# Converting the MoE weights in half-width VectorE steps inside the attention

## The chip, the core and the metric

The kernel runs on one core of a Trainium2 chip. The metric is the time of one execution on the device, in microseconds (us); the profile is one such execution. The core has five engines, each of which takes its instructions strictly in the order in which the program wrote them: TensorE (PE; its weight loads have a row of their own, PEld), VectorE (DVE), ScalarE (ACT), GpSimd (POOL) and SyncE (SP), which here only issues transfers (DMA). An engine that waits for a semaphore holds up all that is queued behind it.

## What is computed

```python
# attention: 2 batches x 8 heads, 768 positions, 64 wide, 16 clusters
q_assign = argmax(normalize(q) @ normalize(c).T); k_assign likewise
mask     = q_assign[:, :, :, None] == k_assign[:, :, None, :]
scores   = where(mask, q @ k.T / 8, -1e9)
attn     = softmax(scores);  x = attn @ v          # (1536, 512) after the heads are joined
# first MoE layer: float64-wide inputs read as given, 512 -> 2048 -> 512
h = x @ w_in;  x = elu(h) @ w_out
# second: 4 experts, 512 -> 1024 -> 512
out = sum_e p[:, e] * (relu(x @ w1[e]) @ w2[e])
```

The weights w_in and w_out come as 64-bit floats. [...]

## The kernel before

The attention runs first, then the two MoE layers. The attention goes over 48 windows w; six windows make a pair of heads, and a window handles two blocks of 128 query rows. All instructions of all windows are sorted by a table of numbers: a step with the name N of window w stands at AT[N] + 4.6 w, plus a correction from SHIFT for the window's place in its pair (w mod 6). This sort is the order in which each engine gets its work; nothing reorders it later. The numbers are units of that table, not microseconds.

The steps of a window that matter here:

- S0, S1: TensorE's scores into PSUM (L364, L367). M0, M1: VectorE's row maximum of each (L373). E0, E1: ScalarE's exponential with the row sum (L382).
- G0, R0: the sum plus 1e-9 (ScalarE, L390) and its reciprocal (VectorE, L394). P0, P1: GpSimd scales the rows by it (L400).
- T0 to T2: TensorE's transposes (L412). C0 to C2: ScalarE's copies to ph, the high part (L425; some to raw, L422). L0 to L2: VectorE's low part pl (L433), in four of 18 cases GpSimd's (L430, L431).
- V0, V1: TensorE's product with v (L441). X0, Y0: one head's half is copied (ScalarE, L453) and added to xs (VectorE, L461). Z0: GpSimd's split of xs (L472, L473).
- Q0 to Q5: the preparation of the next pair (transposes qkps, copies qh and kh L201, low parts L203, cluster logits lps L239 and L240, one-hot rows ohps and ohT L287, and SyncE's transfers of these into the operands QA, QB, KA, KB).
- W0, at 3.79: one step of the weight conversion, from window 3 on.

The conversion (`weights`, L484, and `w_split`, L683) is a generator. Each time do_W is called it runs to the next yield. Two weight chunks are converted inside the attention, each in two halves of 128 x 512 numbers, with one buffer for the raw words (w_raw) and one for the two intermediate tiles (w_tmp). A half's ten steps are: the load by SyncE (L626 or L629); an empty one; Abs of the high words by ScalarE (L702); a clamp by VectorE (L704, TENSOR_SCALAR); a shift with xor by VectorE (L707, TENSOR_SCALAR) with ScalarE's Sign (L708); the low words' three bits shifted in by VectorE (L710, SCALAR_TENSOR_TENSOR); Abs by ScalarE (L714); the sign multiplied back by VectorE (L716, TENSOR_TENSOR); the high part by ScalarE (L718); the low part by GpSimd (L721). The other 14 chunks are converted in the MoE stage, at twice that width, by the same w_split without the small buffers.

Of the kernel before, what the change touches and what calls it, by code (L numbers as in the profile page):

```python
# [8 lines left out]
F32 = mybir.dt.float32  # L9
# [4 lines left out]
AF = mybir.ActivationFunctionType  # L14
ALU = mybir.AluOpType
# [8 lines left out]

PERIOD = 4.6
AT = dict(
    S0=0, M0=0.23, Q0=0.36, Q1=0.85, S1=1.23, Q2=1.45, Q3=1.49, E0=1.75, Q4=3.28, M1=3.78, W0=3.79,
    Q5=4.23, E1=5.04, G0=5.64, R0=6.1, P0=6.11, P1=7.19, T0=10.42, C0=10.63, T1=11, T2=11.5,
    L0=12.79, C1=13.17, C2=13.81, L1=13.84, L2=14.94, V0=17.59, V1=19.11, X0=19.59, Y0=20.28, Z0=20.57,
)  # L30
SHIFT = {
    ("E1", 0): -0.35, ("E0", 1): 1.04, ("V0", 1): 0.84, ("S0", 2): -2.55, ("W0", 2): -3.28, ("G0", 4): 0.41, ("R0", 4): 0.41, ("P0", 4): 0.41,
    ("V1", 4): -1.31, ("W0", 4): 2.64, ("V0", 5): 1.42,
}

POOL_SPLITS = (2, 4, 6, 11)
# [5 lines left out]
TOP = float.fromhex("0x1.cp+16")  # L42
LOW = float.fromhex("0x1.2p-15")
# [3 lines left out]
def kernel(  # L47
# [14 lines left out]
    pe, act, dve, pool, sp = nc.tensor, nc.scalar, nc.vector, nc.gpsimd, nc.sync  # L62
# [28 lines left out]
    def gtile(tag, name, shape, dt):  # L91
        t = gen.tile([128, 1024], dt, tag=tag, name=name)
        n = 1
        for x in shape[1:]:
            n *= x
        if len(shape) == 2:
            return t[:shape[0], :n]
        names = "abcd"[:len(shape) - 1]
        return t[:shape[0], :n].rearrange(
            f"p ({' '.join(names)}) -> p {' '.join(names)}", **dict(zip(names, shape[1:]))  # L100
        )


    def attention():
# [145 lines left out]
        def prep_argmax(j, part, g0=0, g1=4):  # L250

            yield
            yield
            n = g1 - g0
            if part == 0 and g0 == 0:
                oh_t[j] = (
                    am_p.tile([128, T, 4, 1], F32, tag="mx", name="mx"),
                    am_p.tile([128, T, 4, C], F32, tag="rk", name="rk"),
                    am_p.tile([128, T, 4, C], BF16, tag="oh", name="oh"),
                )  # L260
            if n == 4:
                L, mx, rk, oh = (x.rearrange("p t g c -> p (t g) c") for x in (L_t[j], *oh_t[j]))
            else:
                L, mx, rk, oh = (x[:, :, g0] for x in (L_t[j], *oh_t[j]))
            top = mx.to_broadcast([128, T * n, C])
            if part == 0:
                dve.tensor_reduce(out=mx, in_=L, axis=AX.X, op=ALU.max)
                eng = dve if j == 0 else pool
                eng.tensor_tensor(out=L, in0=L, in1=top, op=ALU.subtract)
            elif part == 1:  # L270
                dve.scalar_tensor_tensor(
                    out=rk, in0=L, scalar=0.0, in1=ramp.to_broadcast([128, T * n, C]), op0=ALU.is_ge, op1=ALU.mult
                )
                dve.tensor_reduce(out=mx, in_=rk, axis=AX.X, op=ALU.max)
            else:
                dve.tensor_tensor(out=oh, in0=rk, in1=top, op=ALU.is_equal)
# [31 lines left out]
        def run(*gens):  # L308
            for g in gens:
                for _ in g:  # L310
                    pass
# [172 lines left out]
        def weights(n):  # L484

            for i in range(2):
                raw = cv_p.tile([128, 512, 2], I32, tag="raw", name="w_raw")
                w_load(n, [raw], i)
                yield
                yield  # L490
                tmp = cv_p.tile([128, 2, 512], I32, tag="tmp", name="w_tmp")
                yield from w_split(n, [tmp[:, x] for x in range(2)], i)
# [1 line left out]
        w_gen = [g for n in range(W0) for g in (weights(n),)]  # L494

        def do_W(w, i):
            if w < 3:
                return
            while w_gen:
                if next(w_gen[0], 0) is None:  # L500
                    return
                w_gen.pop(0)
# [34 lines left out]
        for nm in "qk":  # L537
# [7 lines left out]
        NW = NPAIR * 2 * NH  # L545
        do = dict(S=do_S, M=do_M, E=do_E, G=do_G, R=do_R, P=do_P, T=do_T, C=do_C, L=do_L, V=do_V, X=do_XC, Y=do_XA,
                  Z=do_XS, Q=do_Q, W=do_W)

        items = sorted(
# [3 lines left out]
        for at, w, nm in items:  # L553
            if w == 0 and nm == "S0":
                run(*(prep_argmax(0, i, g, g + 1) for i in range(3) for g in (1, 3)))
# [47 lines left out]
    A11, A12, A22, S1, S2, S3, S4 = range(7)  # L603
    W0 = 2
# [8 lines left out]
    def w_tiles(n):  # L613
        return [home(f"{t}{n % NSLOT}", [128, 2, 512], f"w{t}{n % NSLOT}") for t in "hl"]
# [37 lines left out]
    def w2_split(n):  # L652

        st = st_t.pop(n).bitcast(F32).rearrange("p i f t -> p i (f t)")
        a, b = st[:, 0], st[:, 1]
        tags = W2_TAGS[n % 2]
        a = a.rearrange("p (k c f) -> p k c f", k=KD, c=2)
        b11, b12, b21, b22 = (a[:, k:k + 2, c] for k in (0, 2) for c in range(2))
        t = gen.tile([128, 4, 2, 128], F32, tag="kh", name="T")
        dve.tensor_tensor(out=t[:, 0], in0=b12, in1=b11, op=ALU.subtract)  # L660
        dve.tensor_tensor(out=t[:, 2], in0=b22, in1=b12, op=ALU.subtract)
        yield
        dve.tensor_tensor(out=t[:, 1], in0=t[:, 0], in1=b22, op=ALU.subtract)
        dve.tensor_tensor(out=t[:, 3], in0=t[:, 1], in1=b21, op=ALU.add)
        yield
        ops = {}
        for x, names in (
            (a[:, :, 0], ("B11", "B21")), (t[:, 0:2].rearrange("p a k f -> p (a k) f"), ("T1", "T2")),
            (t[:, 2:4].rearrange("p a k f -> p (a k) f"), ("T3", "T4")), (b22, ("B22",)),
        ):  # L670
            m = 2 * len(names)
            o = home(tags[len(ops) // 2], [128, 2, m, 128], "w1op")
            yield from split(o[:, 0], o[:, 1], x, dve)
            for i, nm in enumerate(names):
                ops[nm] = [[o[:, z, 2 * i + kk] for kk in range(2)] for z in range(2)]
            yield
        h, l = (home(tag, [128, 2, 512], "w2op") for tag in tags[4:])
        b = b.rearrange("p (c d) -> p c d", c=2)
        yield from split(h, l, b, dve)
        w_t[n] = ops, (h, l)  # L680
        yield

    def w_split(n, tmp=None, half=None):  # L683
        if chunks[n][0] == 2:
            yield from w2_split(n)
            return
        a = st_t.pop(n)
        if n not in w_t:
            w_t[n] = w_tiles(n)
        h, l = w_t[n]  # L690
        if half is not None:
            h, l = h[:, half], l[:, half]

        small = tmp is not None
        a32, sg = tmp if small else [gtile(("qh", "kl", "kh")[n % 3], "wa", [128, 2, 512], I32), gtile("ql", "wsg", [128, 2, 512], I32)]
        at = (slice(None),) * (len(a.shape) - 1)
        hi, lo = a[at + (1,)], a[at + (0,)]
        x, sg = a32.bitcast(F32), sg.bitcast(F32)  # L700

        act.activation(out=x, in_=hi.bitcast(F32), func=AF.Abs)  # L702
        yield
        dve.tensor_scalar(x, x, LOW, TOP, ALU.max, ALU.min)  # L704
        if small:
            yield
        dve.tensor_scalar(a32, a32, 3, 0x40000000, ALU.logical_shift_left, ALU.bitwise_xor)  # L707
        act.activation(out=sg, in_=hi.bitcast(F32), func=AF.Sign)  # L708
        yield
        dve.scalar_tensor_tensor(  # L710
            out=a32, in0=lo, scalar=29, in1=a32, op0=ALU.logical_shift_right, op1=ALU.bitwise_or
        )
        yield
        act.activation(out=x, in_=x, func=AF.Abs)  # L714
        yield
        dve.tensor_tensor(out=x, in0=x, in1=sg, op=ALU.mult)  # L716
        yield
        act.activation(out=h, in_=x, func=AF.Copy)  # L718
        if small:
            yield  # L720
        pool.tensor_tensor(l, x, h.bitcast(F32), ALU.subtract)  # L721
        yield

    def moe():
# [254 lines left out]
        def tick(t, k=1):  # L979
            for n in start.get(t, ()):  # L980
                w_gen2[n] = w_split(n)
                going.append(w_gen2[n])
            for _ in range(k):
                going[:] = [it for it in going if next(it, 0) is None]
            for n in load_at.get(t, ()):
                w_load(n)
# [68 lines left out]
```

## Time and profile before

| | us |
|---|---|
| median of 3 runs | 1052.17 (1049.82 to 1054.71) |
| the profiled execution | 1049.63 |
| its span, first to last instruction | 1047.9 |
| TensorE busy | 1029.1 |
| VectorE busy | 735.4 |
| ScalarE busy | 524.2 |
| GpSimd busy | 392.8 |
| attention's steady part | 26 to 262 |

The span is what the trace covers; the rest of the execution's time, 1.73 us, lies around it. Busy times are read by stage, since the engines' shares differ from stage to stage. Matmuls are pipelined and their ends are modelled, so a TensorE that is busy isn't one at its peak. The chain of work that ended last is followed back from the last instruction: each piece is what the next one had waited for, or what stood ahead of it on its engine.

### The profile page before, as it was taken

The page shows a single profiled execution, that of the slowest core. Times are in us where ns is not written, and L with a number is a line of the kernel's source. Part 1 is how long each engine was busy: PE and PEld are TensorE (multiplying, and loading weights), DVE is VectorE, ACT ScalarE, POOL GpSimd, SP SyncE. Part 2 cuts the span into 40 slices and gives each one's busy share as a digit, 9 for nine tenths or more (in the row PEclk, how much of TensorE's full clock was granted, in tenths as well). Part 3 has the DMA queues.
Part 4 walks back from the last instruction along what each step waited for, and adds up shares of the span by engine and source line. Part 5 has one row for each costly group of instructions (what it writes and reads, how often), then busy time and mean ns, then how long its engine had stood idle before and what let it go on. Part 6 is the DMA issues. An engine that isn't in the chain of part 4 may idle for free.

```text
span 1047.9 us, 16446 instructions
## 1 busy us (share of the span) xinstructions
PE 1029.1 (98%) x6253; PEld 918.4 (88%) x6253; DVE 735.4 (70%) x1248; ACT 524.2 (50%) x1081; POOL 392.8 (37%) x394
## 2 busy tenths in 40 slices
PE   8999999999999999999999999999999999999998
PEld 7989999989877888888888898999999898989897
DVE  6999989998689674326576765666666767666665
ACT  4989999988676563324442332233332333332331
POOL 2888888889578766344641000000000000000000
PEclk8999999999999999999999999999999999999999
DMA  8746664431323221010002101111101111001003
GB/s 184 186 109 155 144 145 104 111 92 33 114 96 122 81 96 66 1 41 0 1 1 81 41 1 41 41 41 41 35 7 41 41 42 41 17 25 41 1 1 121
DMA packets 61790, 67.53 MB, mean 64 GB/s; under 512 B 29008, under 2 KB 47440, under 8 KB 61712
## 3 DMA queue, kind: packets, MB, share of 16 engines
q1 hardware_dynamic: 61712, 66.49, 22.4%
q8 instruction: 49, 0.80, 0.3%
q14 instruction: 29, 0.24, 0.1%
HBM read 43.08 MB, written 3.15 MB: 44 GB/s over the span
## 4 chain that ended last, share of the span: by engine, by line
PE 84%; DVE 8%; ACT 4%; issue 2%; DMA 1%; SPq 1%; POOL 1%; DVEq 0%; ACTq 0%; POOLq 0%
PE a L915 35%; PE h L765 23%; PE h L745 10%; PE x L441 5%; PE tps L412 4%; PE s L364 2%; PE s L367 2%; DVE pl L433 2%; DVE nm L373 1%; PE lps L239 1%; PE lps L240 1%; DVE wa L710 1%; ACT ph L425 1%; PE qkps L199 1%; ACT e L382 1%
## 5 line engine op out<-in xcount | busy, mean ns | idle before, releaser
L765 PEld LDWEIGHTS h<-x,w1op 128*128 128x128 f32 x2016 | 257.4, 190 | 10.3 <-ACT r L776 1.2
L765 PE MATMUL h<-x,w1op 128*128 128x256 f32 x2016 | 261.2, 285 | 1.0 <-ACT r L776 1.0
L915 PE MATMUL a<-w2op,gh 128*128 128x512 f32 x768 | 238.4, 392 | 0.0
L915 PEld LDWEIGHTS a<-w2op,gh 128*128 128x128 f32 x768 | 138.0, 188 | 23.9
L924 DVE SCALAR_TENSOR_TENSOR acc<-a,prob,acc 128x512 f32<-128x512 f32 x180 | 129.7, 746 | 40.2 <-PE a L915 40.2
L915 PE MATMUL a<-w2op,gl 128*128 128x512 f32 x384 | 149.8, 390 | 0.0
L745 PE MATMUL h<-xT,wh 128*128 128x512 f32 x384 | 118.5, 390 | 0.6 <-DVE gg L754 0.5
L400 POOL TENSOR_SCALAR p<-e,sm 128x768 f32<-128x768 f32 x96 | 88.4, 927 | 40.2 <-DVE sm L394 29.0
L754 DVE SCALAR_TENSOR_TENSOR gg<-r,h 128x512 f32<-128x512 f32 x48 | 32.9, 685 | 96.5 <-ACT r L753 75.4
L373 DVE TENSOR_REDUCE nm<-s 128x1 f32<-128x768 f32 x96 | 90.9, 947 | 2.8 <-PE s L367 2.6
L382 ACT ACTIVATE e<-s,nm 128x768 f32<-128x768 f32 x96 | 86.6, 902 | 4.5 <-POOL p L400 2.8
L412 PE MATMUL tps<-ident,p 128*128 128x128 f32 x576 | 83.5, 277 | 2.9 <-DVE pl L433 2.7
L745 PEld LDWEIGHTS h<-xT,wh 128*128 128x128 f32 x384 | 71.9, 188 | 16.2 <-DVE gg L754 1.4
L776 ACT ACTIVATE r<-h 128x256 f32<-128x256 f32 x48 | 18.4, 384 | 134.8 <-PE h L765 134.8
L915 PEld LDWEIGHTS a<-w2op,gl 128*128 128x128 f32 x384 | 72.1, 188 | 15.6
L433 DVE TENSOR_TENSOR pl<-tps,ph 128x512 fp32r<-128x512 f32 x112 | 76.2, 683 | 6.6 <-ACT ph L425 5.2
L441 PE MATMUL x<-ph,v 128*128 128x256 f32 x288 | 76.6, 298 | 1.4 <-DVE xs L461 1.3
L752 ACT ACTIVATE r<-h 128x512 f32<-128x512 f32 x48 | 28.6, 595 | 97.7 <-PE h L745 96.9
L915 PE MATMUL a<-gh,wh 128*128 128x512 f32 x192 | 74.9, 390 | 1.0 <-ACT acc L931 0.9
L755 POOL TENSOR_SCALAR gh<-gg 128x512 fp32r<-128x512 f32 x48 | 41.0, 854 | 92.0 <-DVE gg L754 89.2
L915 PE MATMUL a<-gl,wh 128*128 128x512 f32 x192 | 74.8, 390 | 0.0
L915 PE MATMUL a<-gh,wl 128*128 128x512 f32 x192 | 74.7, 389 | 0.0
(152 smaller groups left out, 1942.1 us busy)
## 6 DMA issues: line engine op xcount, KB each, us to landing
st<-in_moe_w_dram SPq DMA_DIRECT2D x32, 512.0 KB, 4.3
st<-in_moe_w_in_dram SPq DMA_DIRECT2D x14, 512.0 KB, 3.7
st<-in_moe_w_out_dram SPq DMA_DIRECT2D x14, 512.0 KB, 4.6
QA<-qh SPq DMA_DIRECT2D x32, 192.0 KB, 4.2
nq<-in_q_dram SPq DMA_DIRECT2D x16, 192.0 KB, 3.8
nk<-in_k_dram SPq DMA_DIRECT2D x16, 192.0 KB, 3.9
nv<-in_v_dram SPq DMA_DIRECT2D x8, 384.0 KB, 3.9
QB<-ql SPq DMA_DIRECT2D x16, 192.0 KB, 4.2
```

The lines of the kernel that those rows point to most:

```text
L373: dve.tensor_reduce(out=m_t[w][:, i:i + 1], in_=s_t[HALF * w + i][:, :, 0:384], axis=AX.XY, op=ALU.max, negate=True)
L382: act.activation(out=e, in_=s_t.pop(u)[:, :, 0:384], func=AF.Exp, bias=m_t[w][:, i:i + 1], accum_out=e_t[w][0][:, i:i + 1])
L400: pool.tensor_scalar(p, e_t[w][1 + i].rearrange("p a b -> p (a b)"), e_t[w][0][:, i:i + 1], 1.0, ALU.mult, ALU.mult)
L412: pe.transpose(ps[:, x, :], p_t[w][i][:, c * 128:(c + 1) * 128], ident)
L433: dve.tensor_tensor(out=l, in0=ps, in1=h.bitcast(F32), op=ALU.subtract)
L441: pe.matmul(x_t[w], lhsT=v2[j][:, r, c, :], rhs=t[:, :, c, :], start=(c == 0 and t is ph[w]), stop=(c == T - 1 and t is pl[w]),)
L745: pe.matmul(ps, lhsT=w[:, 0, f], rhs=x, start=(kk == 0 and i == 0), stop=(kk == KD - 1 and i == 2))
L754: dve.scalar_tensor_tensor(out=gg, in0=r, scalar=-1.0, in1=ps, op0=ALU.add, op1=ALU.max)
L755: pool.tensor_scalar(gh, gg, 1.0, 0.0, ALU.mult, ALU.add)
L765: pe.matmul(ps, lhsT=w[wz][kk], rhs=x[xz][:, kk], start=(start and kk + i == 0), stop=(stop and kk == 1 and i == 2), skip_group_check=True,)
L915: pe.matmul(ps, lhsT=x, rhs=y, start=(opens and i == 0), stop=(closes and i == len(ops) - 1))
L924: dve.scalar_tensor_tensor(out=t, in0=ps, scalar=pr, in1=t, op0=ALU.mult, op1=ALU.add)
```

## The change

The four VectorE steps of the small conversion become two each, over columns 0 to 255 and 256 to 511, each with a yield of its own; the ScalarE and GpSimd steps keep their width. A half so has 14 steps. For these, do_W gets two places: W0 at 2.4, in every window, and W1 at 3.85, in odd windows only. The SHIFT entries of the old W0 (for windows 2 and 4 of a pair) now bear the name W1. For the large conversion the list of columns has one entry of 512, as before.

```diff
-    S0=0, M0=0.23, Q0=0.36, Q1=0.85, S1=1.23, Q2=1.45, Q3=1.49, E0=1.75, Q4=3.28, M1=3.78, W0=3.79,
+    S0=0, M0=0.23, Q0=0.36, Q1=0.85, S1=1.23, Q2=1.45, Q3=1.49, E0=1.75, W0=2.4, Q4=3.28, M1=3.78, W1=3.85,
...
         def do_W(w, i):
-            if w < 3:
+            if w < 3 or (i == 1 and w % 2 == 0):
                 return
...
+        cols = [slice(0, 256), slice(256, 512)] if small else [slice(0, 512)]
+
+        def rest():
+            if small:
+                yield
+
         act.activation(out=x, in_=hi.bitcast(F32), func=AF.Abs)
         yield
-        dve.tensor_scalar(x, x, LOW, TOP, ALU.max, ALU.min)
-        if small:
-            yield
-        dve.tensor_scalar(a32, a32, 3, 0x40000000, ALU.logical_shift_left, ALU.bitwise_xor)
-        act.activation(out=sg, in_=hi.bitcast(F32), func=AF.Sign)
-        yield
-        dve.scalar_tensor_tensor(
-            out=a32, in0=lo, scalar=29, in1=a32, op0=ALU.logical_shift_right, op1=ALU.bitwise_or
-        )
-        yield
+        for c in cols:
+            dve.tensor_scalar(x[..., c], x[..., c], LOW, TOP, ALU.max, ALU.min)
+            yield from rest()
+        for c in cols:
+            dve.tensor_scalar(
+                a32[..., c], a32[..., c], 3, 0x40000000, ALU.logical_shift_left, ALU.bitwise_xor
+            )
+            if c is cols[0]:
+                act.activation(out=sg, in_=hi.bitcast(F32), func=AF.Sign)
+            yield
+        for c in cols:
+            dve.scalar_tensor_tensor(
+                out=a32[..., c], in0=lo[..., c], scalar=29, in1=a32[..., c], op0=ALU.logical_shift_right,
+                op1=ALU.bitwise_or,
+            )
+            yield
         act.activation(out=x, in_=x, func=AF.Abs)
         yield
-        dve.tensor_tensor(out=x, in0=x, in1=sg, op=ALU.mult)
-        yield
+        for c in cols:
+            dve.tensor_tensor(out=x[..., c], in0=x[..., c], in1=sg[..., c], op=ALU.mult)
+            yield
```

ScalarE's order around its first Abs of the conversion, in window 4 (the exponential ahead of it is the one that starts at 37.87 in the trace; L709 of the changed kernel is L702 of the one before):

```order
 L422 ACTIVATE raw<-tps 128x512
 L382 ACTIVATE e,sm<-s,nm 128x768
+L709 ACTIVATE w_tmp<-w_raw 128x512
 L201 ACTIVATE qh<-qkps 128x384
 L425 ACTIVATE ph<-tps 128x512 x2
```

Before, this Abs stood nine rows further on, behind the next Copy to qh; SyncE's row for the load that it needs, the first of w_raw, has not moved.

VectorE's order in the stretch that the trace has from 54 to 61 us; before:

```order
L461 TENSOR_TENSOR xs<-x,xt 64x256
L433 TENSOR_TENSOR pl<-tps,ph 128x512
L373 TENSOR_REDUCE nm<-s 128x1
L707 TENSOR_SCALAR w_tmp<-w_tmp 128x512
L245 TENSOR_TENSOR L<-lps,ltmp 128x3x32
L433 TENSOR_TENSOR pl<-tps,ph 128x512
L373 TENSOR_REDUCE nm<-s 128x1
L710 SCALAR_TENSOR_TENSOR w_tmp<-w_raw,w_tmp 128x512
L433 TENSOR_TENSOR pl<-tps,ph 128x512
L245 TENSOR_TENSOR L<-lps,ltmp 128x3x32
L394 RECIPROCAL sm<-sm 128x2
L461 TENSOR_TENSOR xs<-x,xt 64x256
```

And the same stretch of VectorE's order now (L715 is the shift, L707 before; L722 the low words' bits, L710 before):

```order
L461 TENSOR_TENSOR xs<-x,xt 64x256
L715 TENSOR_SCALAR w_tmp<-w_tmp 128x256
L433 TENSOR_TENSOR pl<-tps,ph 128x512
L373 TENSOR_REDUCE nm<-s 128x1
L722 SCALAR_TENSOR_TENSOR w_tmp<-w_raw,w_tmp 128x256
L245 TENSOR_TENSOR L<-lps,ltmp 128x3x32
L433 TENSOR_TENSOR pl<-tps,ph 128x512
L373 TENSOR_REDUCE nm<-s 128x1
L433 TENSOR_TENSOR pl<-tps,ph 128x512
L245 TENSOR_TENSOR L<-lps,ltmp 128x3x32
L394 RECIPROCAL sm<-sm 128x2
L461 TENSOR_TENSOR xs<-x,xt 64x256
```

Two whole steps that followed a row maximum have become one half-step behind the addition to xs (place W0), one half-step behind the row maximum (place W1), and the next half-step again behind the addition to xs, right after the last row shown.

## Rows read from the trace of the kernel before

**Rows 1.** Busy us by stretch (count), granted TensorE clock, DMA share, GB/s
```profile
core 0: us, PE busy (x) PEld busy (x) DVE busy (x) ACT busy (x) POOL busy (x), PEclk, DMA share, GB/s
...
44.50:76.60 32.10, 30.61 (x235) 28.86 (x235) 30.59 (x55) 28.62 (x68) 26.59 (x32) 1.00 0.50 118
...
107.20:137.70 30.50, 30.15 (x234) 29.05 (x234) 28.74 (x54) 28.02 (x67) 27.32 (x32) 1.00 0.52 123
...
26.00:262.00 236.00, 229.03 (x1748) 217.52 (x1748) 217.28 (x389) 212.26 (x493) 205.06 (x241) 1.00 0.50 120
```

**Rows 2.** Timeline of ScalarE: start, us, instruction, [idle before it]
```profile
37.87 0.90 ACT L382 ACTIVATE e<-s,nm 128x768 f32<-128x768 f32 x1
...
38.75 0.49 ACT L201 ACTIVATE qh<-qkps 128x384 fp32r<-128x384 f32 x1
...
40.59 0.90 ACT L382 ACTIVATE e<-s,nm 128x768 f32<-128x768 f32 x1 [0.38 <-DVE nm L373]
...
44.80 0.68 ACT L702 ACTIVATE w_tmp<-w_raw 128x512 f32<-128x512 f32 x1
```

**Rows 3.** SyncE's issue of the first load, and its time to landing
```profile
37.32 0.88 SPq L629 DMA_DIRECT2D w_raw<-in_moe_w_in_dram x1
...
DMA to landing us min/median/max: 5.1/5.1/5.1
```

**Rows 4.** The chain that ended last, 40 to 45 us: start, us, what
```profile
41.58 0.96 ACT ohT L287
42.56 0.36 ACT xt L453
...
43.79 0.70 DVE pl L433
44.54 0.66 PE tps L412 x4
```

**Rows 5.** The same chain: three of the conversion's seven pieces on it
```profile
56.13 0.59 DVE w_tmp L707
...
104.83 1.37 DVE w_tmp L704
...
214.27 1.26 DVE w_tmp L710
```

**Rows 6.** Timeline of VectorE and GpSimd at two steps of the second half
```profile
104.75 1.45 DVE L704 TENSOR_SCALAR w_tmp<-w_tmp 128x512 f32<-128x512 f32 x1
...
104.63 1.29 POOL L431 TENSOR_TENSOR pl<-raw,ph 128x512 fp32r<-128x512 f32 x1
...
113.02 0.68 DVE L710 SCALAR_TENSOR_TENSOR w_tmp<-w_raw,w_tmp 128x512 int32<-128x512 int32 x1
```

**Rows 7.** The same view at the new W0's place, in two windows
```profile
216.40 0.43 DVE L461 TENSOR_TENSOR xs<-x,xt 64x256 f32<-64x256 f32 x1
216.86 0.69 DVE L433 TENSOR_TENSOR pl<-tps,ph 128x512 fp32r<-128x512 f32 x1
...
216.54 0.91 POOL L400 TENSOR_SCALAR p<-e,sm 128x768 f32<-128x768 f32 x1 [1.56 <-DVE sm L394]
...
54.34 0.91 POOL L400 TENSOR_SCALAR p<-e,sm 128x768 f32<-128x768 f32 x1 [3.21 <-DVE sm L394]
```

**Rows 8.** Busy us by stretch at the start (columns as in rows 1)
```profile
10.00:12.00 2.00, 1.91 (x15) 1.81 (x14) 1.19 (x3) 1.07 (x4) 0.84 (x1) 0.90 0.98 214
12.00:14.00 2.00, 2.00 (x11) 2.00 (x11) 0.82 (x4) 0.34 (x2) 0.00 (x0) 0.50 0.99 210
...
18.00:20.00 2.00, 1.65 (x8) 1.32 (x7) 1.86 (x9) 0.00 (x0) 0.00 (x0) 0.89 1.14 233
20.00:22.00 2.00, 1.34 (x15) 1.03 (x16) 1.96 (x6) 1.25 (x3) 0.00 (x0) 1.00 1.08 262
```

**Rows 9.** VectorE's groups by shape: xcount | busy us, mean ns | idle before
```profile
L433 DVE TENSOR_TENSOR pl<-tps,ph 128x512 fp32r<-128x512 f32 x112 | 76.2, 683 | 6.6 <-ACT ph L425 5.2 <-issue 0.7 <-POOL pl L431 0.3
...
L806 DVE SCALAR_TENSOR_TENSOR gl<-gg,gh 128x256 fp32r<-128x256 f32 x48 | 20.4, 425 | 0.0
```

**Rows 10.** The second load of w_raw, issued at 85.46, to landing
```profile
DMA to landing us min/median/max: 7.8/7.8/7.8
```

More of the change, by code (lines that the diff above doesn't have):

```diff
@@ L31 @@
 SHIFT = {
-    ("E1", 0): -0.35, ("E0", 1): 1.04, ("V0", 1): 0.84, ("S0", 2): -2.55, ("W0", 2): -3.28, ("G0", 4): 0.41, ("R0", 4): 0.41, ("P0", 4): 0.41,
-    ("V1", 4): -1.31, ("W0", 4): 2.64, ("V0", 5): 1.42,
+    ("E1", 0): -0.35, ("E0", 1): 1.04, ("V0", 1): 0.84, ("S0", 2): -2.55, ("W1", 2): -3.28, ("G0", 4): 0.41, ("R0", 4): 0.41, ("P0", 4): 0.41,
+    ("V1", 4): -1.31, ("W1", 4): 2.64, ("V0", 5): 1.42,
 }
```

## The prediction

> **What bounds the kernel now.** The chain of work that ended last is mostly TensorE, so I first asked in which stage the edited code runs: only in the attention, from 26 to 262 us. By stretch, TensorE and VectorE are both almost full there: 30.61 and 30.59 us of 32.10 in the second pair of heads, 30.15 and 28.74 us of 30.50 in the fourth [rows 1]. Whoever is held up for long, the end moves. The chain inside the stage then changes hands: long runs of TensorE, and between them stretches where ScalarE and VectorE end last. One of these is the chain from 41.58 to 44.54, three steps of ScalarE and one of VectorE before TensorE goes on [rows 4]. In the others the conversion itself stands on the chain, seven times, from 56.13 to 214.27, with 0.59, 1.26, 1.37, 0.48, 0.73, 0.59 and 1.26 us, 6.3 us in all (first, third and last in [rows 5]). The whole prize is thus some 6 us of 1050, and the rest of the program is unchanged.
>
> **The change, part by part.** Four conversions (two chunks, two halves) are each cut from four VectorE instructions to eight of half the width, and their steps go into three places per two windows instead of one per window.
>
> *Places and loads.* A half has 14 steps now, not 10. The load is step 1 and the first ScalarE step, Abs, step 3. Before, these lay two windows apart; now three places cover two windows, so they can lie one window apart. The first load shows what that means. SyncE issues it at 37.32, and its data take 5.1 us [rows 3], so they are there at 42.46. Its row in SyncE's order is the same in both programs, and no earlier instruction changes, so this time stands. Before, Abs came at 44.80, after the landing, and waited for nothing [rows 2]. Now it stands right behind the exponential that starts at 37.87 and ends at 38.77, ahead of the Copy to qh at 38.75 [rows 2]. **ScalarE then has to wait from 38.77 to 42.46, 3.7 us, and everything queued behind waits with it**: qh, two Copies to ph, the exponential, the one-hot row. Abs itself takes 0.57 us to the next start, so qh starts at 43.03 instead of 38.75, 4.3 us late. Before, ScalarE waited 0.38 us ahead of the exponential at 40.59 for a row maximum [rows 2]; that gap closes, which leaves 3.9 us. From there to 44.54 the chain is ScalarE's own (one-hot 41.58, Copy to xt 42.56, then the subtraction at 43.79), without another gap to close [rows 4]. So TensorE goes on at about 48.4 instead of 44.54: **+3.9 us**. All engines are late by the same from then on, and in two engines that are 94% and more busy there is little to win it back. Bounds: above 4.3 us, if the gap doesn't close; below 0 us, should TensorE have enough stored work, which I reject because ScalarE is what it waits for just there.
>
> The other three loads: the third is issued some ten us before its Abs, and costs nothing. The second is moved ahead of a q or k load by 4 us and its Abs by 10 us; the fourth is moved into the company in which the second had taken 7.8 us [rows 10], while its Abs comes some 7 us after it. Each may wait for up to 1 us in a stretch where TensorE is last. I put them at 0 (hidden by TensorE's own work), 0 to 1.6 us in the range. SyncE's order moves only around these loads; what is moved behind them (k loads, k stacks) is needed a pair later.
>
> *The pieces.* What a conversion instruction costs depends on GpSimd. At 104.75 the TENSOR_SCALAR took 1.45 us: GpSimd had begun a subtraction at 104.63 that ended at 105.92, and the VectorE instruction ended 0.28 us after that. At 113.02, with nothing of the kind in its way, the widest one took 0.68 us [rows 6]. So an instruction that finds GpSimd at work waits for its end, and then runs. Cutting it in two gives two such meetings. And the new place W0 lies badly for this: it comes behind the reciprocal and the addition to xs, and the reciprocal is what GpSimd waits for to begin its 0.9 us product. At 216.83, where the last piece will stand (the addition starts at 216.40, the subtraction at 216.86), GpSimd has begun such a product at 216.54, with 0.62 us to go; at 54.63, where the first half's fourth piece will stand, one began at 54.34 [rows 7]. I put all 32 pieces into the trace of before by their neighbours in VectorE's order: 28 find GpSimd at work, with 14.2 us left in sum, half a microsecond each. The 16 instructions of before waited about 4 us in sum.
>
> Which of it counts? Before, 6.3 us were on the chain. On the same stretches and at 43.85 stand 14 pieces now. Ten of them would meet 5.5 us of GpSimd work (0.2 to 0.76 each; the first and the last are those of [rows 7]). Their own runs are half of the whole instruction's: about 0.16 us for six TENSOR_SCALARs (half of the 0.28 above, and a start) and 0.3 for eight others (half of the 0.68, less the overlap), 3.3 us. They fill 0.5 us in which VectorE waited for ScalarE anyway. That makes 8.3 us against 6.3: **+2.0 us**. Bounds: -2.9 us, if the engines' shift makes all ten meetings disappear; +9 us, if the remaining 18 pieces, which bring some 7 us more of VectorE time, come onto the path too. I take +2.0, because VectorE has 1.8 us free per pair in the stretches of the others (28.74 of 30.50 [rows 1]), and six pairs of that cover 7 us.
>
> An instruction of 512 columns has a row with 683 ns, one of 256 a row with 425 [rows 9]: two halves are 0.17 us more than a whole, 2.7 us for 16 cuts, of VectorE's time, not of the path. [...] By that alone the change would cost these 2.7 us at most; the rows of the pieces above say that the meetings with GpSimd are the larger price.
>
> *Sum.* 3.9 + 2.0 = 5.9 us. The profiled execution took 1049.63 us (1047.90 of span and 1.73 around it), so it would take 1055.5. The median of the runs shown is 1052.17, 2.5 us above that execution, and the sum onto the median gives **1058.1 us**, 0.56% more. (What counts as a difference here is 0.5%, 5.3 us.)
>
> **The rivals.** *The clock falls as well.* TensorE would stand nearly still for some 3 us from 40.8 on. [...] Against it: from 18 to 20 and from 20 to 22 it was busy for 1.65 and 1.34 us of 2 each, and the clock stayed at the full level behind them [rows 8]. [...]
>
> *The wait is absorbed.* If ScalarE and TensorE win back the 3.9 us over the remaining 220 us, only the pieces count: 1052.17 + 2.0 = 1054.2, no difference that counts. For it: each pair has 0.4 to 1.5 us in which TensorE is not busy [rows 1]. Against it: these come from waits for engines that are late by the same.
>
> *Faster.* Shorter instructions let the row maximum and the subtraction behind them start earlier. It needs two things at once: the meetings mostly fall away because everything is shifted (-2.9 us, the lower bound), and the ScalarE wait doesn't reach the end. That gives 1049.3, still within the bound; more than 5.3 us would need all 6.3 us of the chain's conversion to vanish, 1045.9.
>
> *The change doesn't do what it says:* excluded, the order has 16 more VectorE rows, and the even windows' W1 does nothing, so that the two shifts now tied to W1 in windows 2 and 4 are without effect.
>
> **How the numbers follow.** Forecast, wait of 3.9 us and pieces between -1 and +5: 0.55. Clock falls too: 0.15. Wait absorbed: 0.21. Faster by the pieces: 0.09. The predicted time is that of the first, 1058. The range reaches from 1051 (wait absorbed and a little of the gain) to 1064 (clock, with pieces somewhat dearer than taken). Slower by over 5.3 us: two thirds of the first case and nearly all of the second, 0.5. Faster by over 5.3 us: only the extreme of the last case, 0.06. The rest is 0.44.
>
> **What would show it.** ScalarE's first Abs of the conversion starting at about 42.5 with 3.7 us idle ahead of it, put down to the DMA of w_raw; the exponential behind it at about 44.5; TensorE with a hole around 41 to 44, and its granted clock after that. Conversion pieces of 128x256 that take 0.5 us and more in the mean, not half of a whole one's run, and most of the longest right behind the additions to xs. The time from 231 on, and the MoE stage, equal but for the shift. I am wrong if Abs does not wait, if the hole is there but pairs 2 to 7 are shorter than 30.5 to 32 us, or if pieces run in 0.2 to 0.35 us each, which would mean that they slip between GpSimd's instructions.

## The result and the profile after

The changed kernel takes 1064.44 us in the median (five runs, 1063.57 to 1065.32; a sixth, of 5752.76 us, is left out), the kernel before 1053.27 (six runs): a ratio of 1.0106 with the interval 1.0087 to 1.0125, **11.2 us slower**. The prediction said 1058.0 and 1051 to 1064. Its sign is right and the things that it looked for are there, its size is not: the time lies above the range.

The profiled execution took 1064.41 us, with a span of 1062.6. The first thing to look for is ScalarE's first Abs of the conversion, between the exponential and the Copy to qh. The timeline of ScalarE after (start, us, instruction, idle before it), as in [rows 2]:

```profile
43.05 0.66 ACT L709 ACTIVATE w_tmp<-w_raw 128x512 f32<-128x512 f32 x1 [3.96 <-DMA w_raw<-in_moe_w_in_dram]
...
44.94 0.92 ACT L382 ACTIVATE e<-s,nm 128x768 f32<-128x768 f32 x1
```

It waits 3.96 us for the load of w_raw, and the exponential that stood at 40.59 in [rows 2] starts at 44.94. TensorE's timeline has the hole that follows from it:

```profile
40.68 0.28 PE L441 MATMUL x<-pl,v 128*128 128x256 f32 x1
44.73 0.49 PE L282 MATMUL ohps<-identb,oh 128*64 128x128 bf16 x6 [3.78 <-DVE ql L203]
```

The granted clock is lower behind the hole. By stretch after (us, PE, PEld, DVE, ACT and POOL busy, granted clock, DMA share, GB/s; columns as in [rows 1]):

```profile
38.00:44.50 6.50, 2.96 (x23) 2.64 (x21) 3.10 (x6) 2.54 (x7) 4.69 (x5) 1.00 0.58 160
44.50:52.00 7.50, 7.27 (x47) 7.04 (x47) 6.23 (x13) 6.85 (x16) 3.22 (x4) 0.77 0.30 64
```

TensorE was busy for 2.96 of 6.50 us, and the mean clock of the next 7.50 us is 0.77: 3.4 us of them (7.5 x 0.23 / 0.5) at half of the full clock, 0.50 in every half microsecond from 46 to 49.

The second thing is what the pieces take: the halves of the conversion's VectorE steps, which make 32-bit floats of the 64-bit weights. VectorE's groups by shape from 20 to 280 us (line, xcount | busy us, mean ns of one | idle before), after:

```profile
L722 DVE SCALAR_TENSOR_TENSOR w_tmp<-w_raw,w_tmp 128x256 int32<-128x256 int32 x8 | 5.8, 724 | 0.1
L712 DVE TENSOR_SCALAR w_tmp<-w_tmp 128x256 f32<-128x256 f32 x8 | 4.9, 609 | 0.1
L730 DVE TENSOR_TENSOR w_tmp<-w_tmp 128x256 f32<-128x256 f32 x8 | 4.6, 571 | 0.1
L715 DVE TENSOR_SCALAR w_tmp<-w_tmp 128x256 int32<-128x256 int32 x8 | 4.5, 565 | 0.1
```

and the same view of the kernel before:

```profile
L710 DVE SCALAR_TENSOR_TENSOR w_tmp<-w_raw,w_tmp 128x512 int32<-128x512 int32 x4 | 4.2, 1046 | 0.0
L704 DVE TENSOR_SCALAR w_tmp<-w_tmp 128x512 f32<-128x512 f32 x4 | 3.9, 974 | 0.0
L716 DVE TENSOR_TENSOR w_tmp<-w_tmp 128x512 f32<-128x512 f32 x4 | 2.9, 714 | 0.0
L707 DVE TENSOR_SCALAR w_tmp<-w_tmp 128x512 int32<-128x512 int32 x4 | 2.6, 650 | 0.0
```

Half the columns cost 0.57 to 0.72 us where the whole cost 0.65 to 1.05: 19.8 us in sum against 13.6. VectorE's and GpSimd's timeline after show why one piece is quick and another is not:

```profile
212.67 0.27 DVE L715 TENSOR_SCALAR w_tmp<-w_tmp 128x256 int32<-128x256 int32 x1
...
217.37 0.40 DVE L461 TENSOR_TENSOR xs<-x,xt 64x256 f32<-64x256 f32 x1
217.69 1.00 DVE L722 SCALAR_TENSOR_TENSOR w_tmp<-w_raw,w_tmp 128x256 int32<-128x256 int32 x1
218.61 0.68 DVE L433 TENSOR_TENSOR pl<-tps,ph 128x512 fp32r<-128x512 f32 x1
...
217.13 1.27 POOL L431 TENSOR_TENSOR pl<-raw,ph 128x512 fp32r<-128x512 f32 x1
```

The piece at 212.67 finds GpSimd idle and takes 0.27 us. The one at 217.69 stands behind the addition to xs, finds GpSimd in a subtraction that ends at 218.40, and ends 0.29 us after that. Of the 32 pieces 27 find GpSimd with 0.1 us or more of an instruction still to run (14 of 16 before), and the eight longest, 0.75 to 1.00 us, all stand right behind an addition to xs. Five of the 27 are not held up: each starts within 0.1 us of the start of GpSimd's product p and takes 0.27 to 0.42 us, and the product takes 1.04 to 1.19 us in place of 0.91 [rows 7].

Who pays is seen in the chain that ended last, after:

```profile
163.60 0.44 DVE xs L461
...
164.06 0.86 DVE w_tmp L722
...
164.95 0.70 DVE pl L433
...
165.70 0.66 PE tps L412 x4
```

Addition, piece, subtraction, and only then TensorE's transposes. In this profile the chain can be followed back to 124 us. From there to the end of the attention it has 15 pieces of the conversion, 8.5 us in sum; before, it had four behind 124, 3.1 us. The waits of TensorE for that subtraction, from 40 to 270 us (who waited for whom: us, times, longest), after and then before:

```profile
PEld tps L412 <- DVE pl L433: 10.0, 16, 1.2
...
PE tps L412 <- DVE pl L433: 5.9, 13, 1.0
```

```profile
PEld tps L412 <- DVE pl L433: 4.8, 8, 0.9
...
PE tps L412 <- DVE pl L433: 2.7, 6, 0.6
```

Laid side by side, the two profiles run together until window 4, whose first score product starts 0.23 us later after than before (35.48 and 35.25). In window 6 it is 4.88 us late: the hole and the clock. From there the delay grows in small steps, to 8.6 in window 21, 12.1 in window 27, 14.4 in window 42, and the MoE stage adds 0.3. So some 4.7 us come from the wait with its clock, and some 9.9 from what follows. The whole is 14.7 us, and not 11.2: the profile of before is a quicker run than its median. The experiments have to explain that too.

### The profile page after: what moved, and what is told of

It is laid out like the page before. It is cut to its first block, busy times and chain, and to the rows that moved or that the text cites. A ratio compares the mean times of both kernels' runs of the same rounds, so it can differ in the third digit from the quotient of the medians.

```text
span 1062.6 us, 16462 instructions
## 1 busy us (share of the span) xinstructions
PE 1033.1 (97%) x6253; PEld 919.9 (87%) x6253; DVE 742.4 (70%) x1264; ACT 525.7 (49%) x1081; POOL 393.5 (37%) x394
## 4 chain that ended last, share of the span: by engine, by line
PE 72%; DVE 7%; ACT 4%; POOL 3%; issue 2%; ACTq 0%; DVEq 0%; POOLq 0%
PE a L929 35%; PE h L779 23%; PE h L759 10%; PE x L441 2%; PE tps L412 1%; ACT e L382 1%; DVE pl L433 1%; POOL p L400 1%; DVE nm L373 1%; DVE wa L722 1%; PE s L364 1%; ACT ph L425 1%; DVE wa L712 1%; DVE wa L715 1%; PE s L367 1%
## 5 line engine op out<-in xcount | busy, mean ns | idle before, releaser
L412 PEld LDWEIGHTS tps<-ident,p 128*128 128x128 f32 x576 | 65.2, 141 | 13.2 <-DVE pl L433 10.0
```

What stands on the lines that cost most here:

```text
L412: pe.transpose(ps[:, x, :], p_t[w][i][:, c * 128:(c + 1) * 128], ident)
```

## Experiments

**Does ScalarE's wait cost the median run?** Two runs: one moves only the first Abs, in the kernel before, the other only the first load, in the kernel after.

```diff
# first Abs moved (edit of the kernel before; W1 at 2.4)
-            if w < 3:
+            if w < 3 or (i == 1 and w != 4) or (i == 0 and w in (4, 5)):
                 return
+            if w == 4:
+                next(w_gen[0])
# first load earlier (edit of the kernel after)
             for i in range(2):
+                if n == 0 and i == 0:
+                    yield
...
-            if w < 3 or (i == 1 and w % 2 == 0):
+            if w < 2 or (i == 1 and w % 2 == 0):
```

> The kernel before with one edit: ScalarE's first Abs of the conversion stands in window 4 at 2.4, as in the changed kernel; every other instruction of every engine keeps its place. Theory (the wait for the first load reaches the end, and the clock falls behind it): ScalarE idle 3.7 to 4 us ahead of that Abs, 4 to 5.5 us over before. Rival (the wait is absorbed by the rest of the attention): the same idle time, under 1 us over before.

Measured: 1054.3 us, ratio 1.0013 (1.0000 to 1.0026), 0.9 us over its kernel before by medians; the interval reaches from nothing to 2.7 us. The size is the rival's, but neither text expected what its profile shows: Abs waits for nothing.

> The changed kernel with one edit: the first load of w_raw is issued a window earlier (window 2), six rows further ahead in SyncE's order; all else keeps its place. Theory (two separate causes: the wait, and some 9 us from the pieces): the first Abs no longer waits, the granted clock holds, and the time falls by 4 to 5.5 us against the changed kernel, to some 5 to 7 us over before. Rival (the wait put the engines out of step and the later growth follows from it): all 11 us go, within 2 us of before.

Measured: 1064.8 us, ratio 1.0114 (1.0089 to 1.0139). Nothing is won; both theories miss. Its profile has ScalarE's Abs with no wait ahead of it, as has that of the first run; here is load_early's:

```profile
42.67 0.67 ACT L711 ACTIVATE w_tmp<-w_raw 128x512 f32<-128x512 f32 x1
```

ScalarE comes there at 42.67 of its own. All the work is late by then, because TensorE's clock has fallen earlier. The view by stretch of this kernel:

```profile
28.00:36.00 8.00, 8.00 (x35) 8.00 (x35) 3.86 (x8) 4.11 (x11) 3.71 (x6) 0.50 1.11 284
```

and of the kernel before, in its profile:

```profile
12.00:18.00 6.00, 6.00 (x33) 5.29 (x33) 3.34 (x14) 1.30 (x4) 0.00 (x0) 0.50 1.02 215
...
28.00:36.00 8.00, 7.53 (x58) 7.22 (x58) 7.40 (x13) 7.31 (x19) 7.61 (x10) 1.00 1.02 252
```

These eight microseconds hold 58 matmuls in the profile of before and 35 in load_early's. In some runs the clock holds from 20 us on, as in the profile of before; in others it is at half for some 10.2 us between 26 and 38, with TensorE full of work. The runs of before show both: of 53 beside these experiments 12 lie at 1049.4 to 1051.1 us, with a mean clock of 0.996 to 0.998, and 41 at 1053.1 to 1056.2, with 0.992 to 0.995. The profile of before, 1049.63, is of the first group; the median is of the second. No profile of this kernel caught the second course: that its longer runs have it is read from their mean clocks, which 10.2 us at half lower by 0.005. In a run of the second group ScalarE reaches the Abs some 4 us later anyway, when the data have landed: at 42.67 in load_early and 43.56 in lows_back below, against 39.09 in the profile of after. **The wait of 3.96 us and the early fall of the clock exclude each other**, and the median of before already pays the one. Eight profiles have the early fall with the Abs at its new place and the load at its old one; in them the Abs waits for 0.46 us at most:

```profile
44.02 0.67 ACT L715 ACTIVATE w_tmp<-w_raw 128x512 f32<-128x512 f32 x1 [0.46 <-DMA w_raw<-in_moe_w_in_dram]
```

That line is of the run lows_back, below. The times agree. The kernels with the Abs at its old place have short runs: those 12 of before, and one of six and one of eight in two kernels below (halves_old_places, no_steps), some 4 us under the rest. The nine kernels with the Abs at its new place and the load at its old one have none in 65 runs; no two runs of one kernel lie more than 2.1 us apart. One run of abs_early has a mean clock of 0.998, which leaves no room for 10.2 us at half; it took 1055.37 us, 4 to 6 us more than the short runs of before. There the wait seems to be paid in full, but this run has no profile.

**What the pieces cost.** All 32 taken out of the kernel after; all 16 steps out of the kernel before.

```diff
-            dve.tensor_scalar(x[..., c], x[..., c], LOW, TOP, ALU.max, ALU.min)
+            if not small:
+                dve.tensor_scalar(x[..., c], x[..., c], LOW, TOP, ALU.max, ALU.min)
...
# and so for the other three, in either kernel
```

> The changed kernel without the 32 VectorE pieces of the small conversion (the clamp, the shift, the low words' bits and the sign are left out); every other instruction keeps its place. It prices the pieces as a whole. Theory (nearly all of the 11 us comes from the pieces on VectorE): 3 to 6 us under before. Rival (the new places of the ScalarE and GpSimd steps cost a part): still over before.

Measured: 1053.0 us, ratio 0.9998 (0.9986 to 1.0010), level with before, which neither text expected. The pieces cost 11.4 us.

> The kernel before without its 16 VectorE steps of the small conversion (left out: the same four operations). Its distance to before is what the conversion costs there. Theory: 3 to 6 us under before, as the seven steps on the chain add up to 6.3 us, and within 1.5 us of the changed kernel without its pieces. Rival (VectorE's gaps hide it): within 1.5 us of before.

Measured: 1048.9 us, ratio 0.9955 (0.9941 to 0.9969). The whole steps cost 4.75 us, as expected; that the two kernels without VectorE work lie within 1.5 us of each other is a miss. So the conversion's VectorE work is 6.7 us dearer now (give or take some 3 us, by the three intervals), and 4.1 us of the loss are there without any VectorE work.

**Width or place?** The whole steps at the new places (the first of each two; the second stays empty), and the halves, back to back, at the old places.

```diff
# whole steps, new places (edit of after; a None is skipped)
-        cols = [slice(0, 256), slice(256, 512)] if small else [slice(0, 512)]
+        cols = [slice(0, 512), None] if small else [slice(0, 512)]
# halves, old places (edit of before; so for all four steps)
-        dve.tensor_scalar(x, x, LOW, TOP, ALU.max, ALU.min)
+        for c in cols:
+            dve.tensor_scalar(x[..., c], x[..., c], LOW, TOP, ALU.max, ALU.min)
```

> The changed kernel with whole steps: each VectorE step of the small conversion is done in one instruction of 512 columns at the first of its two places, and the second place stays empty; all other instructions keep their order. Theory 1 (the number of meetings with GpSimd costs): 16 instead of 32 of them, VectorE's conversion time falls from 19.8 to some 14 us and the time by 4 to 6 us against the changed kernel. Theory 2 (the new place behind the addition to xs costs, whatever the width): within 1.5 us of the changed kernel.

Measured: 1059.6 us, ratio 1.0067 (1.0043 to 1.0091).

> The kernel before with halves: each VectorE step of the small conversion is done in two instructions of 256 columns, one right behind the other, at its old place; all other instructions keep their order. Theory 1 (the number of meetings costs): up to 16 more meetings, 2 to 6 us over before. Theory 2 (the place costs): VectorE's conversion time grows by under 3 us and the time by under 2 us.

Measured: 1057.9 us, ratio 1.0049 (1.0026 to 1.0072). By medians the new places (those of all engines' steps) cost 6.1 us by themselves and halving 4.5, in sum 10.6 against 11.2 for both: within the intervals the two add up. In the second kernel 24 of 32 halves meet GpSimd, and the multiplication with the sign takes 887 ns for a half, where the whole took 714:

```profile
L729 DVE TENSOR_TENSOR w_tmp<-w_tmp 128x256 f32<-128x256 f32 x8 | 6.8, 887 | 0.0
```

**The meetings alone.** Each piece becomes a row maximum of the same 256 columns, which I expected to run beside GpSimd without waiting for it. The conversion is left out.

```diff
-            dve.tensor_scalar(x[..., c], x[..., c], LOW, TOP, ALU.max, ALU.min)
+            dve.tensor_reduce(out=scr, in_=x[..., c], axis=AX.X, op=ALU.max)
```

> The changed kernel with each of the 32 pieces replaced by a row maximum over 256 columns, which reads one tensor from SBUF and writes one column (the conversion is left out). Places and number are those of the changed kernel; what should be missing is the wait for GpSimd. Theory 1 (the meetings with GpSimd cost): none of the 32 shows a wait, each takes some 0.35 us, and the time falls by at least 6 us against the changed kernel. Theory 2 (an instruction more at these places costs, whatever it meets): it falls by less than 3 us.

Measured: 1059.3 us, ratio 1.0060 (1.0041 to 1.0079), with the pieces at 0.41 us in the mean of each of the four steps (407 to 411 ns), whatever GpSimd does:

```profile
L737 DVE TENSOR_REDUCE scr<-w_tmp 128x1 f32<-128x256 f32 x8 | 3.3, 411 | 0.1
```

VectorE's 19.8 us of pieces fall to 13.1, the time by 5.1, which lies between the two theories. **The meetings cost some 5 us of the 11.4; the other 6.3 are 13.1 us of plain VectorE work at these places.** Half of the pieces, the TENSOR_SCALARs, take 0.27 us alone, less than the row maximum, so the meetings' part may be somewhat larger.

**Is it the place behind the addition to xs?** W0's pieces put ahead of the reciprocal, at 1.48.

```diff
-    ... E0=1.75, W0=2.4, ...
+    ... E0=1.75, W2=1.48, W0=2.4, ...   # W2 runs the pieces, W0 the rest
```

> The changed kernel with the pieces that stand at W0 moved ahead of the reciprocal of the same window (to 1.48 from 2.4); those at W1, and all ScalarE, GpSimd and SyncE steps but two swapped neighbours on ScalarE, keep their place. Theory 1 (the place behind the reciprocal is where GpSimd has just begun its product): fewer and shorter waits, 3 to 6 us under the changed kernel. Rival (the piece now delays the reciprocal and with it GpSimd's product): no gain, or slower.

Measured: 1063.0 us, ratio 1.0095 (1.0071 to 1.0119): only 1.4 us less, which the intervals don't tell from nothing. The pieces sum to 21.5 us there and 23 of them meet GpSimd, now often in its 1.3 us subtraction. Out of one meeting, into another.

**What moves without VectorE?** In the profile without pieces the chain goes over GpSimd in a stretch (128 to 142 us) where before it was TensorE's almost alone:

```profile
131.43 0.74 POOL xT L473
132.18 1.26 POOL wl L739
133.44 1.19 POOL p L400
```

and ScalarE's timeline in that kernel has, behind the product,

```profile
134.66 0.90 ACT L382 ACTIVATE e<-s,nm 128x768 f32<-128x768 f32 x1 [1.50 <-POOL p L400]
```

The conversion's low part (wl, 1.3 us on GpSimd) had moved right ahead of a product that ScalarE's next exponential waits for. Before, its four places were those of W0 in windows 12, 22, 32 and 42, the second and third of them moved by the two SHIFT entries; now W0 and W1 set other places, and the entries, tied to W1, do nothing. So I put only the low parts back, which makes GpSimd's order that of before, row for row.

```diff
-        pool.tensor_tensor(l, x, h.bitcast(F32), ALU.subtract)
+        lows.append(lambda: pool.tensor_tensor(l, x, h.bitcast(F32), ALU.subtract))   # if small
...
+            if i == 2:                         # W2=3.79, SHIFT ("W2", 2): -3.28, ("W2", 4): 2.64
+                if w in (12, 22, 32, 42):
+                    lows.pop(0)()
+                return
```

> The changed kernel without its 32 VectorE pieces (so the weights' conversion lacks the clamp, the shifts and the sign), and with GpSimd's four low parts of it put back to where they stand in the kernel before, so that GpSimd's order is the old one row for row. Without pieces and with the low parts at the new places it took 1053.0, and the kernel before without its steps 1048.9: 4.1 us that no VectorE instruction pays. Theory (the moved low part, 1.3 us long, stands right ahead of a product p that the exponential waits for): 2.5 to 4 us come back, 1049 to 1050.5, and ScalarE's wait for p falls from 4.8 us to about 2.1. Rival (it is ScalarE's moved steps that cost): nothing changes, 1053.

Measured: 1051.4 us, ratio 0.9979 (0.9966 to 0.9991), against 0.9998 with the low parts at their new places: 2.0 us, somewhat less than the theory's 2.5 to 4. The wait of the exponential falls as expected, from

```profile
ACT e L382 <- POOL p L400: 4.8, 5, 1.7
```

to

```profile
ACT e L382 <- POOL p L400: 2.2, 5, 0.7
```

> The changed kernel whole, with GpSimd's four low parts of the conversion put back to where they stand in the kernel before. If the low parts' places cost by themselves, it falls from 1064.4 by what the run without pieces falls by, to 1060.5 to 1062. If the pieces hide that cost (they are late at the same places), it stays within 1 us of 1064.4. If the two add to each other, it falls by more than 4 us.

Measured: 1062.1 us, ratio 1.0077 (1.0062 to 1.0093) against 1.0106: 3.1 us.

> The changed kernel with the VectorE steps whole (512 wide, at the first of each two places, the second empty) and GpSimd's low parts at their old places. With the low parts at the new places it took 1059.6, which is 6.1 over the kernel before. Theory that the low parts cost 2.5 to 4 us in any company: 1055.5 to 1057, the rest being VectorE's steps at worse places. Rival: 1059 and over, the low parts count for nothing, and the 6.1 us are all the places of the VectorE and ScalarE steps.

Measured: 1058.0 us, ratio 1.0037 (1.0024 to 1.0051) against 1.0067: 3.2 us. (The time is 1 us above the one expected. The kernel before had 1054.42 us in this group of runs, so ratios are compared, not times.) In all three companies the low parts' places cost 2 to 3 us. Each of the three differences is only a little larger than its interval; all have the same sign.

The profile with low parts back happens to be a run in which the clock fell early (0.58 from 26 to 36), that of after one in which it held. Window 3's first score product starts 4.1 us later in the former (35.34 and 31.23), window 6's only 0.5 us later (51.16 and 50.63): the early fall and the wait for w_raw, each paid once, come out almost equal. That is the exclusion seen in two traces.

**The account.** By ratios, of 11.2 us: halving 4.2 (lows_back's 1.0077 less whole_lows_back's 1.0037), low parts 3.1, and 3.9 for the other changes of place. By the runs without VectorE work, 2.5 of these 3.9 are there without a VectorE step (0.9979 less 0.9955): ScalarE's and SyncE's moved steps, the first Abs among them with its 0.9. That last part isn't split further, and its interval is about as wide as itself. No version here that converts the weights beats the kernel before. There was little to win: with its VectorE steps of the conversion left out altogether, the kernel before is 0.45% faster.

## Why the prediction was wrong

*ScalarE's wait, +3.9.* As a mechanism it is right: 3.96 us idle (3.7 forecast; the load was issued at 37.50 and landed at 43.02, not at 42.46), the exponential at 44.94 (44.5), TensorE's hole from 41 to 44.7, the delay at the end. **One step that failed is the addition onto the median**; it made the forecast too high, not too low. The sum was made against an execution of 1049.63 and its result set upon 1052.17, as if the 2.5 us between them had nothing to do with the stretch in question. They were a different course of the first 40 us, in which the wait is not there. In the median run this term is 0.9 us as measured (0 to 2.7), not 3.9. An estimate agrees: with the short runs gone, 12 of 53 runs lose 4 us each, 0.9 us in the mean.

*The pieces, +2.0.* **This is the step that put the time above the range, a mis-sized term**: 6.7 us were measured. The prediction's sum had 8.3 us of the conversion on the path now and 6.3 before; the runs show 11.4 and 4.75. What each piece would take was near: 28 meetings forecast, 27 counted, most of the longest behind the additions to xs, means of 0.57 to 0.72 us. What failed is the choice between the bounds. I left the 18 pieces off the chain at nothing, since VectorE had 1.8 us free per pair [rows 1]. That free time isn't at the places where the pieces stand: VectorE's idle time is its wait for ScalarE's xt (6.4 us from 20 to 280 us) and the like, and the piece behind the addition holds up the subtraction that TensorE waits for. The pairs tell it, in the view of [rows 1], after:

```profile
50.60:84.00 33.40, 31.16 (x236) 28.90 (x235) 31.23 (x56) 28.25 (x66) 26.38 (x32) 1.00 0.48 112
...
116.30:149.10 32.80, 30.75 (x235) 28.77 (x235) 29.10 (x54) 27.71 (x66) 27.28 (x32) 1.00 0.55 130
```

These two pairs took 32.10 and 30.50 us before; now 33.40 and 32.80, with VectorE free for 2.2 and 3.7 us in them and the time lost all the same. What came lies nearer to the upper bound of +9 us than to the +2.0 chosen. The estimate from [rows 9] for the cuts alone, 2.7 us at most, points the right way; halving cost 4.2 and 4.5 us here, more than that.

*What was left out.* **The low parts' new places were put at nothing, without a reason.** The prediction noted that the shifts now tied to W1 do nothing, and drew no cost from it. The four new places together cost 2 to 3 us. A GpSimd step of 1.3 us had been moved, and I had looked only at what GpSimd does to VectorE.

*The second and fourth load, 0.* The trace after has no wait for w_raw but the first, 4.0 us once.

*The rivals.* "The clock falls as well" happened in the profiled run, for 3.4 us at half, where the clock of [rows 8] was at half for 6.8 in all. The 1064 at the end of the range had half of those 6.8 us, 3.4, as the price of the clock, an estimate; half of the 3.4 measured is 1.7, and it is inside the 4.7 us of the first hole. My counter-argument, that the full level had held behind 18 to 22 us [rows 8], was no argument: those stretches had TensorE busy for 1.65 and 1.34 of 2 us, this one had a single pause of 3.8. The early fall has no such pause ahead of it: in the ten profiles that have it, TensorE's longest pause in the 12 us ahead of the fall is 1.4 us, and from 20 to 26 us TensorE is idle for 1.1 to 1.8 us in sum. "The wait is absorbed" was the right outcome for the median, at 0.21, but not by slack: by another delay that most runs have. "Faster" had nothing for it.

So a dear term (3.9) was counted where the median hardly pays it, and two others were taken at 2.0 and 0 that cost 6.7 and 2 to 3. Of the 11.2 us, 6.7 (pieces), 2.0 (low parts, priced without pieces so that nothing counts twice) and 0.9 (the Abs) are accounted for; some 1.6 us are left to the other moved steps and the intervals. The forecast came out 6.4 us low: 5.3 in the sum of the terms, and 1.1 because the median of before is 1053.27 over six runs, not 1052.17. Its errors had partly cancelled: the wait was 3.0 us too dear, the pieces 4.7 and the low parts 2 to 3 too cheap.

## What to carry to other kernels

Before a sum from one execution is put onto a median, look at what separates the two: if the runs fall into groups, a wait in the profile may be one that the other group never has. Free time of an engine hides an instruction only where it stands in front of that instruction's place; ask who waits for the next one in the queue. And when a table moves a generator's steps, price every engine's step, above all a long one that comes to stand ahead of what another engine waits for.

## What was unexpected of the hardware

The same program has, by the mean clocks of its runs (0.996 to 0.998, and 0.992 to 0.995), two courses of the clock in its first 40 us: at full from 20 us on, as in the profile of before, or at half for some 10.2 us between 26 and 38, as in ten profiles of its variants (a mean of 0.51 from 26.6 to 37 us without pieces). By their times and mean clocks 12 of 53 runs of the kernel before were of the first kind, and these are about 4 us shorter. In the ten profiles with the early fall TensorE is busy nearly throughout the stretch at half: 10.00 of the 10.00 us from 28 to 38 in abs_early. What decides it, no run here shows: some 3.4 us at half between 10 and 20 us (a mean of 0.83) stood ahead of the one in the kernel without steps and of the other in the one without pieces and with the low parts back.

An elementwise piece of 256 columns on VectorE that GpSimd holds up ends 0.15 us (TENSOR_SCALAR) or 0.28 us (the other two operations) after GpSimd's instruction does, in 22 of the 32 cases after. It took 0.27 to 0.42 us alone and up to 1.00 in company, and 887 ns in the mean at one place against 714 for the whole 512 there. Who comes first counts: the five pieces that start within 0.1 us of GpSimd's product ran as if alone, 0.27 to 0.42 us, and the product took 1.04 to 1.19 us in place of 0.91. A row maximum over the same columns took 0.41 us in the mean at these 32 places, beside the same GpSimd work.
